# Two of 32 zero stores written in 18 pieces each, in a one-core decode kernel with gradients

## The chip, the cores and the metric

The kernel runs on one core of one Trainium2 chip. The metric is device microseconds of a whole execution; the time shown is the median of the runs. One execution was also taken by the hardware profiler, and the times of single instructions and DMAs below come from that one.

## The reference

The reference is a forward step and its gradients. A layer norm of `x` (4 batch rows of 512) feeds two branches, whose results are added to `x`: attention of one query position against a key and value cache, and a gated feed-forward layer. The program returns the sum and the gradients with respect to `x`, both caches and all five weights.

```python
def _A_ref(x, k_cache, v_cache, wq, wo):
    W = min(4096, max(256, Sk // 4))
    k = jnp.repeat(k_cache[:, :, Sk - W:, :], rep, axis=1)
    v = jnp.repeat(v_cache[:, :, Sk - W:, :], rep, axis=1)
    ...
xn = _layernorm(x, axis=-1)
return x + _A_ref(xn, A_k_cache, A_v_cache, A_wq, A_wo) + _B_ref(xn, B_w_gate, B_w_up, B_w_down)
...
_out, _vjp = jax.vjp(_f, A_x, A_k_cache, A_v_cache, A_wq, A_wo, B_w_gate, B_w_up, B_w_down)
_grads = _vjp(grad_out)
```

The caches have the shape 4 x 8 x 4096 x 128 (batch, kv-heads, positions, head size) in bfloat16. Only the last 1024 positions of each are used. The gradients of the caches have the full shape, so for the first 3072 positions they are zeros, and these zeros have to be written: 768 KB for each kv-head of each batch and cache, 64 such heads in all, of 81 MB of outputs.

## The kernel before

The kernel first does the feed-forward layer with its weight gradients, then attention batch by batch (scores against K, dP against V, the gradients of V and K, the part of the output and of dq), and last the gradients of `wo` and `wq`. Compute works on tiles in SBUF. Results are copied from PSUM into staging tiles of 1 MB (`stg`, four buffers; late in the kernel also `late` and `last`, on the place of cache tiles) and stored from there.

All large DMAs are issued by SP, in the order in which the kernel's text calls them (`manual_schedule` with `nc.sync.engine`). On that one queue stand:

- the loads of weights (lines 148 and 299 to 302), and of the caches by `load_kv` (line 259): one batch of K or V as two DMAs of 1 MB
- the result stores by `result` (line 109), of 896 KB or 1 MB
- two stores of 4 KB (line 878) for the output and the gradient of `x`
- 32 zero stores by `zeros` (line 277), of 1.5 MB each

A zero store writes the zeros of two kv-heads (`ZG = 2`) of one batch and cache. Each head is seen as 64 rows (`ZP`) of 12 KB (`ZW` = 6144 elements). The source `zsrc` is every second partition of `ztile`, a tile of zeros filled once (line 217), with a step of 0 over the heads. `ztodo` lists the stores, `zdone` those issued. `zeros(n)` issues n of them; `behind` makes each one wait for the landing of the zero store four before it.

Where zero stores stand among the others is written out by hand: `before` (line 105) gives, for each result store, how many zero stores are issued ahead of it, and lines 430, 432, 696 and 717 issue some between the loads of the caches. Numbered from 0 as in `zdone`, store 8 is issued at line 696 for batch 0, right after the two loads of V for batch 1 and ahead of the two loads of K for batch 2 (line 716). Store 29 is issued by `result` ahead of the sixth of the eight stores of weight gradients at the end. After it come that sixth store (1 MB), zero store 30, the seventh, zero store 31 and the eighth.

The framework gives SP's DMAs completion counters in turn, eight in all. An instruction that uses a counter waits until the DMA that last used it has landed, unless an earlier wait covers that.

Of the kernel before, what the change touches and what calls it, by code (L numbers as in the profile page):

```python
# [19 lines left out]
def kernel(  # L20
# [24 lines left out]
    nc = tc.nc  # L45
# [7 lines left out]
    K0 = Sk - W  # L53
# [53 lines left out]
    def result(out, in_):  # L107
        zeros(min(before.popleft(), len(ztodo)))
        return nc.sync.dma_start(out=out, in_=in_)
# [104 lines left out]
    ZP = P // 2  # L214
    ZW = K0 // ZP * Dh
# [48 lines left out]
    ZG = 2  # L264
    zsrc = bass.AP(tensor=ztile.tensor, offset=ztile.offset, ap=[[2 * ztile[:].ap[0][0], ZP], [0, ZG], [1, ZW]])
    ztodo = [(og, b, g) for b in range(B) for g in range(0, G, ZG) for og in (out_2, out_3)]
    zdone = []

    def behind(ins, other):
        tc.add_manual_dep(ins, other.name,  # L270
                          mybir.DependencyInfo(mybir.DependencyClass.Sync, mybir.DependencyReason.DATA))

    def zeros(n, after=None, deep=4):

        for _ in range(n):
            og, b, g = ztodo.pop(0)
            z = nc.sync.dma_start(out=og[b, g:g + ZG, 0:K0, :].rearrange("g (m j) d -> m g (j d)", m=ZP), in_=zsrc)
            if len(zdone) >= deep:
                behind(z.ins, zdone[-deep].ins)
            if after is not None:  # L280
                behind(z.ins, after.ins)
            zdone.append(z)
# [139 lines left out]
    with tc.tile_pool(name="mid", bufs=1, reuse_waits="tile") as mid:  # L422
# [4 lines left out]
        with (tc.tile_pool(name="kvp", bufs=1, reuse_waits="tile") as kvp,  # L427
              tc.tile_pool(name="att", bufs=1, reuse_waits="tile") as att):
            load_kv(0, 1, kvp, "va", nc.sync)
            zeros(2)  # L430
            load_kv(1, 0, kvp, "kb", nc.sync)
            zeros(3)


# [126 lines left out]
            def small(name, shape=(P, 1)):  # L561
                return att.tile(list(shape), FP32, name=name, tag=name)
# [77 lines left out]
            for b in range(B):  # L640
                S = sps[0][:]
                m = small("m")
# [122 lines left out]
            for i in range(KH):  # L765
                t, e, c = i // 8, i // 4 % 2, i % 4
# [144 lines left out]
```

## Time and profile before

| what | value |
|---|---|
| median of 3 runs | 276.65 us (276.42 to 276.9) |
| profiled execution | 276.85 us |
| its span | 275.1 us |
| busy PE, DVE, ACT, POOL | 171.7, 175.8, 122.1, 30.7 us |
| DMA | 24432 packets, 111.88 MB, mean 407 GB/s |
| HBM read, written | 30.68 MB, 81.01 MB |
| zero stores | 32 of 1.5 MB, median 18.3 us from issue to landing |
| store 8, store 29 | issued at 90.48 and 240.93 us |
| last instruction of a compute engine in the chain of waits | ends at 236.45 us |

The span is the time from the first to the last event of the profile; the execution's time has 1.75 us around it. A DMA's issue on SP is a row of its own (engine SPq); the transfer itself runs on the 16 DMA engines, and is seen in the rows of DMA share and GB/s, as packets (a row of a transfer is one packet), and in the landings. A DMA over 16 engines completes once on each of them, and has landed with the last.

### The profile page before, as it was taken

The page shows a single profiled execution, that of the slowest core. Times are in us where ns is not written, and L with a number is a line of the kernel's source. Part 1 is how long each engine was busy: PE and PEld are TensorE (multiplying, and loading weights), DVE is VectorE, ACT ScalarE, POOL GpSimd, SP SyncE. Part 2 cuts the span into 40 slices and gives each one's busy share as a digit, 9 for nine tenths or more (in the row PEclk, how much of TensorE's full clock was granted, in tenths as well). Part 3 has the DMA queues.
Part 4 walks back from the last instruction along what each step waited for, and adds up shares of the span by engine and source line. Part 5 has one row for each costly group of instructions (what it writes and reads, how often), then busy time and mean ns, then how long its engine had stood idle before and what let it go on. Part 6 is the DMA issues. An engine that isn't in the chain of part 4 may idle for free.

```text
span 275.1 us, 3144 instructions
## 1 busy us (share of the span) xinstructions
PE 171.7 (62%) x1095; PEld 57.4 (21%) x1095; DVE 175.8 (64%) x332; ACT 122.1 (44%) x246; POOL 30.7 (11%) x91
## 2 busy tenths in 40 slices
PE   1257988878247668937788778987979956200000
PEld 0121341123023212313223322341112311000000
DVE  7879669988887497515784498619996688300000
ACT  2343674940202766543675556647574455300000
POOL 8500005251152011200000000000000000000000
PEclk9985885558855955555555555555595575555555
DMA  7999989999999999999999999999999999999993
GB/s 267 435 472 401 434 338 421 429 423 403 425 403 436 407 415 415 409 412 402 406 408 433 400 417 417 429 406 431 418 420 407 417 416 429 423 424 421 421 426 152
DMA packets 24432, 111.88 MB, mean 407 GB/s; under 512 B 1361, under 2 KB 1377, under 8 KB 18785
## 3 DMA queue, kind: packets, MB, share of 16 engines
q1 hardware_dynamic: 24408, 111.69, 99.5%
q8 instruction: 8, 0.13, 0.2%
q14 instruction: 8, 0.06, 0.0%
q10 hardware_dynamic: 8, 0.00, 0.0%
HBM read 30.68 MB, written 81.01 MB: 406 GB/s over the span
## 4 chain that ended last, share of the span: by engine, by line
PE 27%; DVE 17%; ACT 7%; DMA 6%; issue 4%; DVEq 0%; ACTq 0%
DVE scr L94 8%; DMA out_dram<-stg 6%; PE kv_ps L131 5%; PE dw_ps L131 4%; PE od_ps L131 4%; PE sc_ps L131 3%; ACT stg L114 2%; PE ok_ps L131 2%; DVE dqs L728 2%; DVE stg L114 2%; ACT late L114 2%; PE dxq_ps L131 1%; DVE wq_t L94 1%; PE dn_ps L131 1%; PE ob_ps L131 1%
## 5 line engine op out<-in xcount | busy, mean ns | idle before, releaser
L114 ACT CAST stg<-kv_ps 128x512 bf16<-128x512 f32 x102 | 54.6, 601 | 41.0 <-PE kv_ps L131 34.1
L131 PE MATMUL sc_ps<-scr,bd 128*32 128x256 bf16 x256 | 19.6, 399 | 17.1 <-DVE scr L94 16.7
L131 PE MATMUL kv_ps<-qm,spr 64*128 64x512 bf16 x64 | 24.3, 582 | 2.2 <-DVE stg L114 0.8
L131 PE MATMUL kv_ps<-dyBD,spr 64*128 64x512 bf16 x64 | 20.7, 584 | 3.4 <-ACT stg L114 3.3
L94 DVE STREAM_TRANSPOSE scr<-va 128x1024 uint32<-128x1024 uint32 x16 | 19.5, 1224 | 0.0
L114 DVE CAST stg<-kv_ps 128x512 bf16<-128x512 f32 x10 | 6.6, 689 | 16.0 <-PE kv_ps L131 16.0
L131 PEld LDWEIGHTS <-spr 64*128 64x128 bf16 (+1 forms) x192 | 9.2, 106 | 29.4 <-issue 25.0
L612 DVE SCALAR_TENSOR_TENSOR odt<-od_ps,om,odt 128x128 f32<-128x128 f32 x12 | 4.2, 351 | 15.6 <-ACT odt L607 15.4
L131 PEld LDWEIGHTS <-bd 128*32 128x32 bf16 x256 | 6.3, 106 | 34.2 <-issue 33.4
L89 ACT CAST stg<-dwg_ps 128x448 bf16<-128x448 f32 x26 | 11.9, 571 | 3.0 <-DVE scr L94 1.9
L114 DVE CAST stg<-dw_ps 128x512 bf16<-128x512 f32 x16 | 10.5, 685 | 4.2 <-PE dw_ps L131 4.0
L131 PE MATMUL dw_ps<-scr,xn_b 32*128 32x512 bf16 x32 | 9.6, 546 | 5.7 <-ACT late L114 4.0
L114 ACT CAST late<-dw_ps 128x512 bf16<-128x512 f32 x16 | 9.2, 587 | 8.5 <-PE dw_ps L131 8.5
L131 PE MATMUL do_ps<-scr,dyBD 128*128 128x512 bf16 x32 | 10.6, 472 | 2.4 <-DVE scr L94 2.3
L114 DVE CAST late<-dw_ps 128x512 bf16<-128x512 f32 x16 | 10.6, 678 | 1.8 <-PE dw_ps L131 1.7
L114 ACT CAST stg<-dw_ps 128x512 bf16<-128x512 f32 x16 | 8.9, 588 | 5.9 <-PE dw_ps L131 5.3
L94 DVE STREAM_TRANSPOSE scr<-wo_sb 128x1024 uint32<-128x1024 uint32 x8 | 9.7, 1230 | 1.3 <-ACT scr L465 0.7
L94 DVE STREAM_TRANSPOSE scr<-ka 128x1024 uint32<-128x1024 uint32 x8 | 9.8, 1234 | 0.8 <-PE r_ps L131 0.7
L94 DVE STREAM_TRANSPOSE scr<-kb 128x1024 uint32<-128x1024 uint32 x8 | 9.9, 1240 | 0.1
L520 POOL COPY bd<-D3d 32x64 bf16<-32x64 bf16 x32 | 7.0, 231 | 23.7 <-DVE D3d L94 11.4
L520 POOL COPY bd<-D3q 32x64 bf16<-32x64 bf16 x32 | 7.2, 239 | 19.6 <-PE sc_ps L131 15.9
L131 PE MATMUL dw_ps<-dy_b,scr 32*128 32x512 bf16 x32 | 8.5, 528 | 1.0 <-ACT late L114 0.7
(200 smaller groups left out, 314.7 us busy)
## 6 DMA issues: line engine op xcount, KB each, us to landing
out_dram<-ztile SPq DMA_DIRECT2D x32, 1536.0 KB, 18.3
out_dram<-stg SPq DMA_DIRECT2D x18, 1024.0 KB, 16.2
va<-in_A_v_cache_dram SPq DMA_DIRECT2D x8, 1024.0 KB, 12.9
out_dram<-stg SPq DMA_DIRECT2D x6, 896.0 KB, 8.5
wq_sb<-in_A_wq_dram SPq DMA_DIRECT2D x1, 4096.0 KB
wo_sb<-in_A_wo_dram SPq DMA_DIRECT2D x1, 4096.0 KB
ka<-in_A_k_cache_dram SPq DMA_DIRECT2D x4, 1024.0 KB, 12.7
kb<-in_A_k_cache_dram SPq DMA_DIRECT2D x4, 1024.0 KB, 15.6
```

The costliest lines, as they stand in the source:

```text
L89: return nc.scalar.copy(out=out, in_=in_)
L94: nc.vector.transpose(out=out, in_=in_)
L114: return nc.scalar.copy(out=out, in_=in_) if eng == "act" else nc.vector.tensor_copy(out=out, in_=in_)
L131: nc.tensor.matmul(out, lhsT=lhsT, rhs=rhs, start=first, stop=last, **kw)
L520: nc.gpsimd.tensor_copy(out=t_[q, :, :, g2, :, o_:o_ + 4], in_=src[q, b, g2])
L612: STT(out=t_[:], in0=ps[:, g, :], scalar=(om, oms)[k][:, g:g + 1], in1=t_[:], op0=ALU.mult, op1=ALU.add)
L728: nc.vector.tensor_copy(out=dqs[q, :, :, :, a * B + b], in_=d3v[q])
```

## The change

In `zeros`, the stores that find 8 or 29 entries in `zdone` are cut. The first DMA then covers one kv-head, g, with its 64 rows of 12 KB. The other head, g + 1, is written as one contiguous stretch of 768 KB, from its start, by 17 further DMAs: 48 rows of 12 KB, 16 rows of 8.25 KB (4224 elements), and 15 DMAs of 15, 14, ... 1 rows of 512 bytes (256 elements). The bytes written are the same. The waits that `behind` adds stay on the first DMA, which is also the one noted in `zdone`. All other zero stores are as before.

```diff
             og, b, g = ztodo.pop(0)
-            z = nc.sync.dma_start(out=og[b, g:g + ZG, 0:K0, :].rearrange("g (m j) d -> m g (j d)", m=ZP), in_=zsrc)
+            cut = len(zdone) in (8, 29)
+            z = nc.sync.dma_start(out=og[b, g:g + ZG - cut, 0:K0, :].rearrange("g (m j) d -> m g (j d)", m=ZP),
+                                  in_=zsrc[:, 0:ZG - cut, :])
+            if cut:
+                head = og[b, g + 1, 0:K0, :].rearrange("k d -> (k d)")
+                at = 0
+                for n, w in [(48, ZW), (16, 4224)] + [(k, 256) for k in range(15, 0, -1)]:
+                    nc.sync.dma_start(out=head[at:at + n * w].rearrange("(m e) -> m e", m=n), in_=zsrc[0:n, 0, 0:w])
+                    at += n * w
+                assert at == ZP * ZW
             if len(zdone) >= deep:
                 behind(z.ins, zdone[-deep].ins)
```

In the built program the 17 DMAs stand on SP right behind the first one, and take the completion counters in turn like all others. The DMAs behind them move on to other counters.

## The prediction

> **What bounds the kernel now.** I read the slices of the page first, then its queues, then busy times by stretch, then SP's issues and waits.
>
> ```profile
> DMA  7999989999999999999999999999999999999993
> GB/s 267 435 472 401 434 338 421 429 423 403 425 403 436 407 415 415 409 412 402 406 408 433 400 417 417 429 406 431 418 420 407 417 416 429 423 424 421 421 426 152
> ...
> q1 hardware_dynamic: 24408, 111.69, 99.5%
> ```
>
> The 16 DMA engines are full from the second slice to the last but one, nearly all with SP's queue. No compute engine passes 64% of the span.
>
> ```profile
> core 0: us, PE busy (x) PEld busy (x) DVE busy (x) ACT busy (x) POOL busy (x), PEclk, DMA share, GB/s
> ...
> 90.00:106.00 16.00, 10.44 (x88) 3.62 (x85) 11.22 (x21) 11.15 (x24) 2.10 (x8) 0.71 1.02 410
> 106.00:122.00 16.00, 11.32 (x85) 3.98 (x84) 7.73 (x20) 7.83 (x19) 1.85 (x8) 0.50 1.04 416
> ...
> 241.00:260.00 19.00, 0.00 (x0) 0.00 (x0) 0.00 (x0) 0.00 (x0) 0.00 (x0) 0.50 1.01 424
> 260.00:268.00 8.00, 0.00 (x0) 0.00 (x0) 0.00 (x0) 0.00 (x0) 0.00 (x0) 0.50 1.00 420
> 268.00:275.00 7.00, 0.00 (x0) 0.00 (x0) 0.00 (x0) 0.00 (x0) 0.00 (x0) 0.50 0.40 167
> ```
>
> Around both changed stores the DMA share is 1.0 or above, and from 241 us on nothing but DMA runs. There is no DMA idle time in which new idle time could hide. The 0.40 of the last 7 us is the engines finishing at different times: the trace's completion records of the last store run from 269.19 to 274.26 us, 5.07 us apart. The latest engine sets the end.
>
> ```profile
> start us, us, engine line op out<-in xcount [idle before <-releaser]
> 89.14 1.29 SPq L259 DMA_DIRECT2D va<-in_A_v_cache_dram  x2
> 90.48 2.80 SPq L277 DMA_DIRECT2D out_dram<-ztile  x1
> 93.38 2.91 SPq L259 DMA_DIRECT2D ka<-in_A_k_cache_dram  x2
> 96.33 6.83 SPq L277 DMA_DIRECT2D out_dram<-ztile  x1
> ```
>
> ```profile
> 228.46 0.28 SPq L878 DMA_DIRECT2D out_dram<-scr  x1
> 231.00 0.26 SPq L878 DMA_DIRECT2D out_dram<-bd  x1
> 234.71 0.61 SPq L277 DMA_DIRECT2D out_dram<-ztile  x1
> 237.28 0.36 SPq L109 DMA_DIRECT2D out_dram<-late  x1
> 240.93 0.61 SPq L277 DMA_DIRECT2D out_dram<-ztile  x1
> 243.40 0.36 SPq L109 DMA_DIRECT2D out_dram<-late  x1
> ```
>
> ```profile
> SPq L277 <- DMA out_dram<-ztile: 14.1, 4, 4.1
> ```
>
> Counting zero stores from 0, number 8 is issued at 90.48 us and number 29 at 240.93. The last row says what SP waits for late in the kernel: landings of older zero stores. SP's DMAs use eight completion counters in turn, and in the built program each waits, before it is issued, for the landing of the DMA eight before it on the same counter. Store 29 shows it: store 26, eight DMAs earlier, landed at 240.91 us, 0.02 before the issue. So at most eight DMAs are queued. In before these are 1 MB to 1.5 MB each, some 9 MB or over 20 us of work, and the queue never runs empty.
>
> **The change, part by part.** The bytes do not change. For stores 8 and 29 each, one DMA (1.5 MB) becomes 18: 0.75 MB, 576 KB, 132 KB, and fifteen of 7.5 KB down to 0.5 KB. That is 34 more DMAs. Order and number of instructions on PE, DVE, ACT and POOL stay.
>
> *The work of the rows.* Packet records give 84 ns for a 2 KB row, 460 ns for a 12 KB row and 9 ns for a counter's increment; the line through the two rows is 9 ns + 36.7 ps per byte. I estimate from it 319 ns for 8.25 KB and 28 ns for 512 bytes. An engine's part of the old store was 8 x 460 + 9 = 3.69 us. Now its large rows cost 7 x 460 + 319 + 3 x 9 = 3.57 us, 0.12 less, and each small store that uses the engine adds 28 + 9 = 37 ns. No 512-byte row is in the trace. If it cost as much as a 2 KB row, the engine with 15 of them would have 15 x 93 = 1.40 us instead of 0.56; at no cost, 0.14. These run while the queue is otherwise empty (next part), so I count them at nothing. Without that cover the engine with all 15 is 0.56 - 0.12 = 0.44 us later per split.
>
> *The counters.* Here I expect the cost. Call the small stores by their rows, 15 to 1. Stores 15 to 10 wait for earlier large DMAs. Store 9 is on the counter of the 48-row piece and store 8 on that of the 8.25 KB piece. Both can only be issued when that piece has landed on all 16 engines. At that moment nothing large is queued: everything older has landed, and behind it stand only rows of 512 bytes. SP must still issue 8, 7, ... 1 before the next large transfer, and that one waits for store 8's landing too. The next large transfers are the ka loads for batch 2 after store 8, and the sixth weight store (`late`) after store 29.
>
> The empty time of the latest engine per split, measured against before, in which its next row follows at once: 0.12 us gained in the rows; 0.33 us from its last packet to the landing (273.93 to 274.26 at the end of the kernel); 0.02 us to wake SP; eight small issues; and the start of the next transfer. The nearest issues are the 4-row ones, 0.28 and 0.26 us at L878, with some 0.05 us between neighbours. I take 0.33 each: 8 x 0.33 = 2.6 us. The lower end is 8 x 0.31 = 2.5, the upper 8 x 0.61 = 4.9 (the 4-row load on ACT's queue took 0.56). For the start, the kernel's first load is the only one into empty engines:
>
> ```profile
> 0.80 0.39 SPq L148 DMA_DIRECT2D wg_sb<-in_B_w_gate_dram  x1
> ```
>
> ```profile
> 1.00:1.50 0.50, 0.00 (x0) 0.00 (x0) 0.00 (x0) 0.10 (x1) 0.42 (x4) 1.00 0.00 0
> ```
>
> Its first packet starts at 1.82 us: 1.0 us (0.6 after the issue ended; up to 1.4 for later engines). Sum: -0.12 + 0.33 + 0.02 + 2.6 + 1.0 = 3.85 us, from 3.3 to 6.6. A gain is excluded while the queue does run empty. The landing of store 8 can take the place of the issues: the 4-row load on ACT's queue landed 2.6 us after its issue began, just the eight issues, so it adds nothing.
>
> *The engines' lateness.* A drain lets early engines wait for the latest. At store 8's landing they are 3.50 us apart, at store 29's 5.10. After a drain all start together, and the time is the sum of the worst engine of each stretch instead of the worst sum. The latest engine gains 5.10 - 3.50 = 1.60 us between the stores; if the second latest there (2.90) is the one at 4.87 later, it gains 1.97, and the drain costs 0.37 more. I take 0.4 (0 if one engine is worst in all stretches, 1.5 if the engine at 1.76 becomes that at 4.87).
>
> *Behind the waits on SP:* ka for batch 2, then zero store 9, then the first result stores (103.27 us before), whose staging buffers ACT waits for (until 121.02 us in the chain of waits). All shift with the queue by the same 3.85 us; a second cost would need SP to run dry, and at its later issues 6 us or more of transfers are queued.
>
> *Total:* 276.85 + 2 x 3.85 + 0.4 = 284.95 us, where 276.85 us is the profiled execution (span 275.1 and 1.75 around it), 0.2 above the median of 276.65. I say 284.9.
>
> **Rivals.**
>
> *One drain is absorbed.* If the compute that runs ahead during the first drain shortens later gaps, one drain counts: 276.85 + 3.85 + 0.4 = 281.1. For it: ACT and PE run on during the first. Against: the share of 1.0 leaves no gap to shorten.
>
> *The round trips are exposed.* If a small landing into HBM takes 5 us and not 2.6 (the L878 stores took 18 and more, behind other work), the next large transfer waits 2.4 us longer per split: 284.95 + 4.8 = 289.7. Against: the engines are empty then.
>
> *Not slower: the fall evens out the engines.* If the queue stays fed, only the rows count. Were the latest engine one that gets none of the small rows, it would save 0.12 us per split: 276.85 - 0.24 = 276.6. It decides from the point where some large transfer is still queued when store 8 is issued. Were it the engine that gets all 15: 276.85 + 0.88 = 277.7. For it: the row counts 15 to 1 are a ramp over engines. Against: the order of counters; and after the store that ended at 249.47 us on its latest engine, the 4-row store of L878 ended at 249.64, so the latest engine is one of the four that it used. [...]
>
> **How the numbers follow.** Two drains 0.73 (own range 283 to 288); one absorbed 0.10; exposed round trips 0.08; queue fed, engines relieved 0.06, or loaded 0.03. The range 281 to 289.5 leaves out the two queue-fed cases and about half of the exposed one. A change under 0.2% (0.55 us) can't be told from none here. Faster 0.02 (the relief larger than worked out), same 0.05, slower 0.93.
>
> **What would show it.** In the changed profile: two dips of the DMA share, near 105 to 110 and near 263 to 267 us, each about 4 us on the latest engine; SP waiting at the small stores for landings of ztile; eight small issues in a row at about 0.33 us right ahead of ka and `late`; busy times of PE, DVE and ACT as before; completions of the last store closer together than 5.07 us. Wrong if the DMA share stays 1.0 there, if the small issues take much less than 0.3 us, or if a dip lasts past the next large issue.

## The result, and the profile after

| kernel | median | of runs | ratio to before |
|---|---|---|---|
| before | 276.53 us | 4 (276.37 to 276.90) | |
| changed | 298.60 us | 4 (298.36 to 299.13) | 1.0791 [1.0775, 1.0807] |

The change costs 22.1 us. The forecast was 284.9 us with a range of 281 to 289.5, so the sign was right and the size was short by 13.7 us. The profiled execution of the changed kernel took 298.47 us, with a span of 296.8 us, 21.7 us more than before.

The page of the changed kernel first: busy times, then the busy share of the DMA engines and GB/s in 40 equal slices (7.42 us each), then SP's queue.

```profile
PE 174.9 (59%) x1095; PEld 57.9 (19%) x1095; DVE 176.4 (59%) x332; ACT 121.9 (41%) x246; POOL 30.6 (10%) x91
...
DMA  7999999999999906999999999999999999993297
GB/s 285 431 451 425 372 407 427 430 412 398 406 436 409 360 18 204 371 421 406 404 397 432 402 418 410 427 407 438 408 425 396 427 422 423 423 411 90 99 425 327
...
q1 hardware_dynamic: 24952, 111.69, 93.4%
```

There are two holes. One begins near 104 us and one near 267 us, and between them the engines are full as before. SP's queue moves the same 111.69 MB, but its packets fill 93.4% of the span where they filled 99.5%. The compute engines do nearly the same work: DVE is busy 0.6 us longer and PE 3.2 us, of 296.8.

The same view in short stretches, with columns as in the table by stretches of the prediction (start and end, length, busy time of PE, PEld, DVE, ACT and POOL, granted clock, DMA share, GB/s):

```profile
104.00:106.00 2.00, 1.75 (x13) 0.28 (x5) 1.10 (x2) 1.30 (x3) 0.92 (x4) 0.50 0.11 37
106.00:108.00 2.00, 1.51 (x9) 0.34 (x12) 1.97 (x5) 1.07 (x3) 0.00 (x0) 0.50 0.03 8
...
110.00:112.00 2.00, 1.83 (x20) 0.74 (x12) 1.15 (x3) 2.00 (x7) 0.92 (x4) 0.50 0.01 2
112.00:114.00 2.00, 1.79 (x25) 0.53 (x17) 1.77 (x7) 2.00 (x6) 0.45 (x2) 0.50 0.09 27
114.00:118.00 4.00, 3.45 (x22) 1.39 (x23) 1.52 (x6) 0.20 (x1) 0.46 (x2) 0.50 0.95 324
118.00:122.00 4.00, 0.00 (x0) 0.00 (x0) 0.00 (x0) 0.00 (x0) 0.00 (x0) 0.93 0.99 314
266.00:270.00 4.00, 0.00 (x0) 0.00 (x0) 0.00 (x0) 0.00 (x0) 0.00 (x0) 0.50 0.83 228
270.00:274.00 4.00, 0.00 (x0) 0.00 (x0) 0.00 (x0) 0.00 (x0) 0.00 (x0) 0.50 0.09 25
274.00:278.00 4.00, 0.00 (x0) 0.00 (x0) 0.00 (x0) 0.00 (x0) 0.00 (x0) 0.50 0.02 5
278.00:282.00 4.00, 0.00 (x0) 0.00 (x0) 0.00 (x0) 0.00 (x0) 0.00 (x0) 0.50 0.48 194
```

Both holes are some 10 us wide at their base and nearly empty for over 6 us. Two further stretches matter. From 114 to 122 us the DMA engines are busy (0.95 and 0.99), yet move only 324 and 314 GB/s. From 266 to 270 us, ahead of the second hole, they move 228 GB/s at a share of 0.83. A busy share is not throughput: the 12 KB rows begun from 266 to 269 us took a mean of 758 ns, where their median before is 460, and the 2 KB rows from 118 to 122 us a mean of 120 ns, where those from 100 to 113 us before took 86.

SP's issues of the changed kernel, columns as before (start, duration with the waits in it, line, operation). L278 is the first DMA of a zero store and L284 the 17 pieces.

```profile
88.55 5.00 SPq L278 DMA_DIRECT2D out_dram<-ztile  x1
93.60 18.96 SPq L284 DMA_DIRECT2D out_dram<-ztile  x17
112.67 0.95 SPq L259 DMA_DIRECT2D ka<-in_A_k_cache_dram  x2
```

```profile
252.67 0.50 SPq L278 DMA_DIRECT2D out_dram<-ztile  x1
255.12 24.20 SPq L284 DMA_DIRECT2D out_dram<-ztile  x17
279.44 0.36 SPq L109 DMA_DIRECT2D out_dram<-late  x1
```

The pieces hold SP for 19 and 24 us, and the next large transfer is issued only behind the last of them, at 112.67 and 279.44 us. What SP waits for between 245 us and the end:

```profile
SPq L284 <- DMA out_dram<-ztile: 5.3, 3, 3.0
SPq L284 <- DMA out_dram<-stg: 3.8, 2, 1.9
```

These are landings of older DMAs, so the counters do hold back the small stores. The last wait is that of the 9-row store, for the landing of the 48-row piece: that came at 273.02 us, the issue began at 273.04. The 8.25 KB piece landed at 273.35, while this issue was still running, so the 8-row store did not have to wait for it. What comes after is not waiting but issuing. The issues of L284 from 107 to 112.5 us, with their number, shortest, median and longest duration in ns:

```profile
L284 SPq DMA_DIRECT2D out_dram<-ztile x9: 424/707/747, 106.3 to 112.1; - x9
```

A small issue takes 0.7 us. The prediction had 0.33 from one issue to the next.

From the completion records of the latest engine, the 21.7 us of the span are these. "Pieces" is the time to the landing of the 8.25 KB piece against the same bytes before; "restart" is from the issue of the next large transfer to a later landing (of zero store 9, or of the last store), against before.

| part | first cut | second cut |
|---|---|---|
| pieces | 4.58 - 3.67 = 0.91 | 6.03 - 3.70 = 2.33 |
| store of 9 rows, issued last before the eight | 0.51 | 0.48 |
| eight small issues | 112.67 - 107.07 = 5.60 | 279.44 - 273.83 = 5.61 |
| restart | 12.65 - 9.85 = 2.80 | 16.31 - 14.81 = 1.50 |
| sum | 9.82 | 9.92 |

Between the cuts another 2.20 us are lost, the start gains 0.45 and the tail loses 0.17: 9.82 + 9.92 + 2.20 - 0.45 + 0.17 = 21.7 us.

### The profile page after: what moved, and what is told of

Same layout as the page of the kernel before. It is cut to its first block, busy times and chain, and to the rows that moved or that the text cites. A ratio compares the mean times of both kernels' runs of the same rounds, so it can differ in the third digit from the quotient of the medians.

```text
span 296.8 us, 3178 instructions
## 1 busy us (share of the span) xinstructions
PE 174.9 (59%) x1095; PEld 57.9 (19%) x1095; DVE 176.4 (59%) x332; ACT 121.9 (41%) x246; POOL 30.6 (10%) x91
## 3 DMA queue, kind: packets, MB, share of 16 engines
q1 hardware_dynamic: 24952, 111.69, 93.4%
## 4 chain that ended last, share of the span: by engine, by line
PE 23%; DMA 15%; DVE 13%; ACT 6%; issue 2%; SPq 1%; ACTq 0%; DVEq 0%
DMA out_dram<-stg 15%; DVE scr L94 6%; PE dw_ps L131 5%; PE kv_ps L131 4%; PE od_ps L131 3%; PE ok_ps L131 2%; ACT stg L114 2%; DVE dqs L737 2%; DVE stg L114 2%; PE sc_ps L131 2%; ACT late L114 2%; PE dxq_ps L131 1%; PE ob_ps L131 1%; PE dn_ps L131 1%; DVE wq_t L94 1%
## 5 line engine op out<-in xcount | busy, mean ns | idle before, releaser
L131 PE MATMUL kv_ps<-dyBD,spr 64*128 64x512 bf16 x64 | 21.4, 607 | 12.1 <-ACT stg L114 12.1
L131 PE MATMUL kv_ps<-qm,spr 64*128 64x512 bf16 x64 | 25.0, 601 | 2.1 <-DVE stg L114 0.8
L89 ACT CAST stg<-dwg_ps 128x448 bf16<-128x448 f32 x26 | 11.9, 567 | 3.0 <-DVE scr L94 1.9
L114 DVE CAST late<-dw_ps 128x512 bf16<-128x512 f32 x16 | 10.8, 682 | 3.4 <-PE dw_ps L131 3.3
L131 PE MATMUL do_ps<-scr,dyBD 128*128 128x512 bf16 x32 | 10.0, 443 | 2.5 <-DVE scr L94 2.3
L131 PE MATMUL dw_ps<-dy_b,scr 32*128 32x512 bf16 x32 | 9.2, 576 | 1.0 <-ACT late L114 0.7
L529 POOL COPY bd<-D3q 32x64 bf16<-32x64 bf16 x32 | 7.2, 238 | 22.1 <-PE sc_ps L131 18.4
```

The lines of the kernel that those rows point to most:

```text
L89: return nc.scalar.copy(out=out, in_=in_)
L114: return nc.scalar.copy(out=out, in_=in_) if eng == "act" else nc.vector.tensor_copy(out=out, in_=in_)
L131: nc.tensor.matmul(out, lhsT=lhsT, rhs=rhs, start=first, stop=last, **kw)
L529: nc.gpsimd.tensor_copy(out=t_[q, :, :, g2, :, o_:o_ + 4], in_=src[q, b, g2])
```

## The experiments

In the diffs, which are shortened, `LOOP` stands for the list after `for n, w in`, and "..." for what is left out. Lines with "-" are those of the changed kernel. Ratios are to the kernel before, run on the same chip (medians 276.55 to 276.74 us).

**One cut at a time.** Are the two drains independent, or is one absorbed?

```diff
-cut = len(zdone) in (8, 29)
+cut = len(zdone) in (29,)      # only29
+cut = len(zdone) in (8,)       # only8
```

> Only store 29 is cut. Theory (each split empties the queue and then pays for itself): the second split's part of the changed kernel's trace, from the landing of the DMA before store 29 to the end, is 9.9 us longer than before, so 276.5 + 9.9 = 286.4 us. Rival (the splits are not independent: the second is dear because the first has used up lateness or buffers): clearly less than 9 or more than 11 us over before.

> Only store 8 is cut. Theory: 9.4 us up to the landing of zero store 9 and 2.2 us more by the time of store 28, because the engines are level after the drain and fall apart again: 276.5 + 11.6 = 288.1 us. Rival (the 2.2 us belong to the second split): 276.5 + 9.4 = 285.9 us.

Measured: only29 287.48 us, 1.039 [1.037, 1.0411]; only8 288.54 us, 1.0429 [1.0407, 1.045]. The costs are 10.8 and 11.9 us, and their sum of 22.7 is within 0.7 of the 22.1 of both. only29 is 1.1 us above the 286.4 expected; by the completion records of its trace 0.8 of that is its pieces, which took 3.1 us more than the same bytes before, not 2.3. Neither drain is absorbed, though PE, DVE and ACT go on working in the first.

**One DMA for all short rows.** Same rows and bytes, but 4 DMAs per cut instead of 18, so that the counters are not used up by small ones.

```diff
-LOOP = [(48, ZW), (16, 4224)] + [(k, 256) for k in range(15, 0, -1)]
+LOOP = [(48, ZW), (16, 4224), (120, 256)]     # 120 rows from ztile[0:n, 0:w]
```

> Both stores are cut, but the 120 rows of 512 bytes are one DMA, so each split has 4 DMAs and not 18. Theory (eight counters full of tiny stores empty the queue): the queue stays fed, the DMA share stays near 1, and at most the slow rows of the 48-row and 8.25 KB pieces remain (0.9 and 2.3 us): 276.5 to 279.7 us. Rival (the short rows and unequal pieces cost by themselves): 290 us or more, with the same dips.

Measured: 282.01 us, 1.0183 [1.0158, 1.0209]. The drain is gone, so the number of small DMAs makes it. But 5.3 us stay, more than the theory allowed: something in the large pieces costs time without a drain. From 254 to 258 us of the profiled execution (283.97 us, the longest of the four) the table by stretches says so (share and GB/s are the last two columns):

```profile
254.00:258.00 4.00, 0.00 (x0) 0.00 (x0) 0.00 (x0) 0.00 (x0) 0.00 (x0) 0.50 1.00 304
```

The engines are full and move 304 GB/s, where 420 is usual.

**Rows over all 16 engines.** Is a small issue slow because its rows don't divide over 16 engines? In the changed kernel's trace a store of n rows, n from 15 to 1, has n completion records; the piece of 16 rows and every larger DMA have 16.

```diff
-LOOP = ... + [(k, 256) for k in range(15, 0, -1)]
+LOOP = ... + [(16, 128)] * 15
```

> The 15 small stores of each split have 16 rows of 256 bytes each, the same bytes in all. Theory (a small store costs SP 0.7 us when it directly follows another, whatever its rows): 298.6 us within 1. Rival (the 0.7 us come from using fewer than 16 engines or a number of rows that is no power of two): the issues fall to the 0.4 us of large DMAs in a row, eight of them save 2.4 us per split, 293.8 us.

Measured: 297.52 us, 1.0753 [1.0726, 1.078]. The issues from 106 to 111.7 us:

```profile
L284 SPq DMA_DIRECT2D out_dram<-ztile x9: 508/587/1130, 105.6 to 111.1; - x9
```

Still 0.59 us each. The row count is not what makes them slow, or only 0.1 us of it.

**Small stores from neighbouring partitions.** `zsrc` steps over every second partition. Here only the small stores' source changes; number, bytes and targets stay.

```diff
-in_=zsrc[0:n, 0, 0:w]
+in_=zsrc[0:n, 0, 0:w] if n > 15 else ztile[0:n, 0:w]
```

> As the changed kernel, but the small stores read neighbouring partitions of the zero tile and not every second one. Theory (a small issue is dear because its source steps over partitions: stores from ztile issue in 0.5 to 0.6 us alone, the 120-row store with neighbouring partitions in 0.34): the issues fall from 0.70 to about 0.4 us, eight of them save 2.4 us per split, 293.8 us. Rival (back to back, the descriptor maker itself needs 0.6 to 0.7 us for each DMA): no change, 298.6 us within 0.5.

Measured: 291.65 us, 1.0538 [1.0507, 1.0568]. The issues from 106.3 to 109 us:

```profile
L285 SPq DMA_DIRECT2D out_dram<-ztile x8: 251/285/294, 106.3 to 108.6; - x8
```

An issue falls from 0.71 to 0.285 us, and eight of them take 2.64 us, just the term of the prediction. The kernel gains 7.0 us: 2 x (5.60 - 2.64) = 5.9 from the eight, the rest mostly from the ninth. The source with the step makes the slow issue; this is the largest part of what the prediction missed. The one-row store, which has no second partition to step to, still took 0.42 us against 0.25 here, so a part goes with how the source is described and not with the partitions that are read; no run separates that part. The expectation had the direction, but too small a gain.

**Half as many small stores, and the cut without a clump.** `eight15` has 8 stores of 15 rows per cut instead of 15 stores. `spread8` cuts store 8 only, and issues its small stores one at a time, each ahead of one of SP's next 15 DMAs.

```diff
-LOOP = ... + [(k, 256) for k in range(15, 0, -1)]
+LOOP = ... + [(15, 256)] * 8                  # eight15
```

```diff
+    def one_more():                           # spread8; called ahead of each later DMA on SP
+        if small_:
+            o_, i_ = small_.popleft()
+            nc.sync.dma_start(out=o_, in_=i_)
...
-                    nc.sync.dma_start(out=..., in_=zsrc[0:n, 0, 0:w])
+                    if n > 15: nc.sync.dma_start(out=one[0], in_=one[1])
+                    else: small_.append(one)
```

> The 120 rows of each split are eight stores of 15 rows and not fifteen of 15 to 1. Theory (the empty time is the issues left to SP when the last large piece lands): only the eighth small store and the next large DMA are left then, seven issues of 0.7 us less per split, 298.6 - 9.8 = 288.8 us. Rival (once the queue has run empty most of the cost is there, whatever the count): over 294 us.

> Only store 8 is cut, into the same 18 pieces, but its 15 small stores are issued one at a time ahead of SP's next 15 DMAs. Theory (small stores cost only where eight in a row fill the counters): no drain; what stays is the slow rows of the large pieces, up to half of what one_small showed, and some 0.2 us for each small store on the latest engine at the most: 277 to 281 us. Rival (each small store costs its issue and its place on a counter wherever it stands): 288 us as with the small stores in a row.

Measured: eight15 288.26 us, 1.0415 [1.0379, 1.0451]; spread8 279.4 us, 1.0091 [1.0067, 1.0115]. Both as the theory had it. SP's issues in eight15 (first row: all ten pieces) and the table by stretches of spread8:

```profile
93.92 13.33 SPq L284 DMA_DIRECT2D out_dram<-ztile  x10
107.36 1.03 SPq L259 DMA_DIRECT2D ka<-in_A_k_cache_dram  x2
```

```profile
104.00:112.00 8.00, 7.10 (x45) 2.04 (x46) 7.10 (x14) 6.54 (x15) 1.40 (x7) 0.50 1.02 404
112.00:120.00 8.00, 4.37 (x38) 1.73 (x39) 2.41 (x11) 1.38 (x5) 0.92 (x4) 0.50 1.04 414
```

With eight small stores ka goes out at 107.36 us instead of 112.67. With the same 15 small stores apart from each other the DMA share stays above 1.0 and 404 GB/s flow where the changed kernel had its hole. So the clump of small stores makes the drain, not their number, rows or slow issue. How many in a row it takes, between one and eight, was not tried.

**What is wrong with the large pieces?** Four kernels ask it. `two_heads` writes the second head as one DMA of 64 rows; `halves` cuts into two DMAs of 32 rows in both heads; `one_home` lets the 48 and the 16 rows read from 16 partitions eight apart; `shape48` writes the second head as 48 and 16 rows of 12 KB, with nothing small.

```diff
-LOOP = [(48, ZW), (16, 4224)] + [(k, 256) for k in range(15, 0, -1)]
+LOOP = [(64, ZW)]                             # two_heads
+LOOP = [(48, ZW), (16, ZW)]                   # shape48
```

```diff
+half = bass.AP(..., ap=[[4 * step, ZP // 2], [0, ZG], [1, ZW]])                # halves
+nc.sync.dma_start(out=og[b, g:g + ZG, 0:K0 // 2, :]..., in_=half)
+z = nc.sync.dma_start(out=og[b, g:g + ZG, K0 // 2:K0, :]..., in_=half)
```

```diff
+rows = bass.AP(..., ap=[[8 * step, 16], [0, 3], [1, w]])                       # one_home, 48 rows
+rows = bass.AP(..., ap=[[8 * step, 16], [1, w]])                               # one_home, 16 rows
```

> Both stores are cut into two DMAs only, one of 64 rows of 12 KB for each head; nothing small, nothing unequal. Theory (with all engines inside one head's 768 KB, the writes get in each other's way): rows of 500 to 1500 ns around both stores and 2 to 5 us over before, 279 to 282 us. Rival (the 48-row and 8.25 KB shapes are at fault, or the small rows): 276.7 us within 0.4.

> Both stores are cut into two DMAs, each with 32 rows of 12 KB in both heads, so that every DMA spans two heads as in before. Theory (one head at a time is what slows the rows): 276.7 us within 0.4. Rival (any cut of a store, or a source with other partitions, does it): as two_heads.

> [...] Theory (the 48- and 16-row pieces are slow because several engines read the same few partitions): the slow rows go, 276.7 to 277.5 us. Rival (they are slow by where they write or by unequal pieces): 282 us as before.

> Both stores are cut into 64 rows of 12 KB for one head, and 48 and 16 rows of 12 KB for the other; no row is short. Theory (16 engines read 48 or 16 rows out of fewer partitions than in the 64-row stores, and so get in each other's way): rows of 600 to 1500 ns around both stores, 279 to 282 us. Rival (the rows of 512 bytes are what slows the others): 276.9 us within 0.5, as two_heads.

Measured: two_heads 277.08 us, 1.002 [1.001, 1.0029]; halves 276.73 us, 1.0008 [0.9998, 1.0017]; one_home 282.19 us, 1.02 [1.0158, 1.0243]; shape48 282.19 us, 1.0207 [1.0181, 1.0233]. A second large DMA costs next to nothing, so the theory for two_heads fell. The same 64 rows as 48 + 16 cost 5.6 us with no small store in the kernel. The tables by stretches of shape48, then of two_heads:

```profile
248.00:252.00 4.00, 0.00 (x0) 0.00 (x0) 0.00 (x0) 0.00 (x0) 0.00 (x0) 0.50 1.01 424
252.00:256.00 4.00, 0.00 (x0) 0.00 (x0) 0.00 (x0) 0.00 (x0) 0.00 (x0) 0.50 1.04 355
256.00:260.00 4.00, 0.00 (x0) 0.00 (x0) 0.00 (x0) 0.00 (x0) 0.00 (x0) 0.50 0.99 341
```

```profile
252.00:256.00 4.00, 0.00 (x0) 0.00 (x0) 0.00 (x0) 0.00 (x0) 0.00 (x0) 0.50 1.00 418
256.00:260.00 4.00, 0.00 (x0) 0.00 (x0) 0.00 (x0) 0.00 (x0) 0.00 (x0) 0.50 1.00 421
```

Both are full, at 341 and at 421 GB/s: the rows of shape48 themselves are slower. one_home was meant to mend this and failed: that the slow rows would go was worked out from the author's assumption of which engine reads which partitions, and no trace here shows that. Its packets tell more: 29 of the 202 rows of 12 KB from 251 to 263 us took 905 to 971 ns, twice the usual 460, and from 255 to 259 us it moved 288 GB/s at a share of 0.97. one_small writes the same rows to the same places from other partitions, and there 9 of 196 rows took 900 to 1000 ns and 16 longer, up to 2281. So the times of the rows changed with the partitions that they are read from. In halves, whose 32 partitions lie four apart over all 128, no 12 KB row from 248 to 262 us took over 500 ns. Why 48 and 16 rows from every second partition are slow (341 GB/s in shape48) and so are the rows from 16 partitions eight apart (288 GB/s in one_home), while 64 from every second (421 GB/s in two_heads) and 32 from every fourth are not, is not shown. Nor does any run keep the number of rows and change their partitions to reach the usual rate, so a part that the number of rows in a DMA has by itself is not ruled out.

**The large pieces from 64 partitions.** `rows64one` is one_small with the large pieces as 64 rows of 9 KB and 64 rows of 2.1 KB; `unit64` is unit with the same pieces.

```diff
-LOOP = [(48, ZW), (16, 4224)] + ...
+LOOP = [(64, 4608), (64, 1056), (120, 256)]                                   # rows64one
+LOOP = [(64, 4608), (64, 1056)] + [(k, 256) for k in range(15, 0, -1)]        # unit64
```

> As one_small, with the 48 rows of 12 KB as 64 of 9 KB and the 16 of 8.25 KB as 64 of 2.1 KB, so that all large rows come from the partitions of an uncut store; the 120 rows of 512 bytes stay one DMA. Theory (few source partitions): 276.9 us within 0.6. Rival (the 512-byte rows): 281 to 282.5 us as one_small.

> As with neighbouring partitions for the small stores, and the large pieces as 64 rows each. Theory (the pieces' slow rows cost 1.5 to 2.4 us of the 15 that are left): 289.7 us, 0.8 either way. Rival (the slow rows come with the small ones): 291.6 us within 0.5.

Measured: rows64one 277.38 us, 1.0033 [1.002, 1.0046]; unit64 288.59 us, 1.0435 [1.0414, 1.0455]. In place of the 304 GB/s of one_small, rows64one shows

```profile
254.00:258.00 4.00, 0.00 (x0) 0.00 (x0) 0.00 (x0) 0.00 (x0) 0.00 (x0) 0.50 1.01 403
```

and loses 0.8 us instead of 5.3. Within the drained kernel the shape is worth 291.65 - 288.59 = 3.1 us, more than expected by 1.1. In unit64's own completion records the pieces take 3.64 and 3.66 us, where the same bytes took 3.67 and 3.70 before, and the eight issues 2.67 and 2.64. What unit64 still loses, 12.0 us, is the drain at the issue price of the prediction.

**The large pieces over both heads.** `clean` wrote the large pieces over both heads at once (64 and 96 rows), 16 rows beside them, and the small stores from neighbouring partitions.

```diff
+z = both_heads(0, K0 // 2, 32)
+both_heads(K0 // 2, K0 - 240, 48)
+nc.sync.dma_start(out=og[b, g, K0 - 240:K0, :]..., in_=zsrc[0:16, 0, 0:1920])
...
+for n in range(15, 0, -1):
+    nc.sync.dma_start(out=..., in_=ztile[0:n, 0:256])
```

> Both stores are cut into 18 pieces, but the large pieces span both heads and the 15 small stores read neighbouring partitions. Theory (what is left is the drain as the prediction worked it out, 2.6 + 1.3 us per split, with the slow loads of 1.5 and the engines falling apart again for 2.2 us): 276.7 + 7.8 + 3.7 = 288.2 us, 1 either way. Rival (the pieces' shapes never mattered): 291.7 us as with neighbouring partitions alone.

Measured: 291.3 us, 1.0532 [1.0511, 1.0553], the rival's number. It still reads 48 and 16 partitions, and so doesn't separate the shape from the rest; unit64 was made for that.

**The slow loads after the first drain.** In the changed kernel the two ka loads, 2 MB, took 7.9 us from first packet to landing, where 5.3 is usual on most engines (6.2 on the latest engine for the same two loads before). `swap8` cuts store 8 only and issues zero store 9 ahead of ka.

```diff
-    load_kv(b + 2, 0, ...)
     zeros(1 - b)
+    load_kv(b + 2, 0, ...)
```

> Only store 8 is cut, as in only8, and zero store 9 stands ahead of the two ka loads behind the split. Theory (loads of 2 KB rows are slow while all engines run level after the drain: 8 us for 2 MB instead of 5.3): the loads stay slow behind a zero store, 288.5 us within 0.7. Rival (only the first transfer into the empty engines is slow): the loads take 5.3 us, some 1.5 to 2.5 us less in all, 286 to 287 us.

Measured: 289.05 us, 1.0451 [1.043, 1.0471]. The total is the one expected, but not for the reason given: the ka loads ran at 2.74 and 2.73 us per MB, nearly as usual, and now zero store 9 took 5.6 us from first packet to landing instead of 3.7 (these times from the first packet hold some 0.3 us from the last packet to the landing, which the usual ones, from landing to landing, do not). So it is not the loads: the first 1.5 to 2 MB after the first drain are slow, whatever they are. After the second drain the rows of the 1 MB store of `late` took their usual 0.31 us. Compute goes on during the first drain and not during the second, but it does not explain this: from 118 to 122 us of the changed kernel no compute engine is busy, and the rate is still 314 GB/s. The cause stays open.

## Why the prediction was right in kind and wrong in size

- **The counters.** Right. The small stores wait for landings, nothing large stands behind them, the DMA engines run empty twice, and SP then issues eight small stores before the next large transfer. spread8 and one_small take the clump away and with it the drain.
- **The step that failed: "I take 0.33 each: 8 x 0.33 = 2.6".** A small issue took 0.70 us and the eight 5.60, beyond even the upper end of 4.9 given for them. The row it was taken from, a 4-row store from neighbouring partitions, was the wrong neighbour: in unit, with such sources, the eight took 2.64 us as predicted, against 5.60 from every second partition. The signs were in the same timeline: zero stores, which read the same `zsrc`, were issued in 0.61 us, and the 1 MB stores of `late` in 0.36. That row was quoted and used only as a bound. Worth 3.0 us per cut, and 0.5 more for the ninth store, which SP issues when the large pieces are nearly or wholly done. The unit run puts both at 7.0 us. With these 7.0 the sum would have been 292 us, still 6.6 short: three smaller parts, below, were short or missing.
- **The rows of the large pieces: "0.12 less" per cut.** Also failed, and wrong in sign. The 319 ns from the line through 2 KB and 12 KB rows is the median of the 8.25 KB rows (mean 371, up to 1187), but the 12 KB rows from 266 to 269 us, the 48-row piece and what ran beside it, took a mean of 758 ns and not 460. shape48 shows 5.6 us for the shape alone; in the drained kernel it is 3.1 us (unit to unit64). That the empty time hides the difference is the author's reading of these two numbers; no run shows it by itself.
- **The 512-byte rows.** Right: a median of 31 ns (27 to 100, 240 rows) against 28. A small store costs the latest engine some 0.18 us with its completion, not 0.037, but hidden in the drain, as was said: at the second cut the last completions of the 8.25 KB piece and of the stores of 15 to 10 rows stand at 273.35, 273.54, 273.72, 273.90, 274.09, 274.28 and 274.46 us.
- **The restart, 1.0 us.** Right: ka's first packet starts at 113.73 us, 1.07 after its issue began. The second cut's restart of 1.50 us is the 1.35 of the prediction (1.0 + 0.33 + 0.02). The first cut's 2.80 has 1.5 us more, the slow first transfers, which the prediction didn't have.
- **The lateness, 0.4 us.** Right in kind, too small, and beyond its upper end of 1.5: the engines leave the first drain level (0.48 us apart at the landing of zero store 9), fall apart again to 2.79 at store 28, and 2.20 us are lost on the way. The mean of the 16 engines took only 0.34 us longer over this stretch than before, so it is the latest engine that loses.
- **The claim that the latest engine is one of the four of a 4-row store** fits before, where it was read (four completion records, the last at 249.64 us), and does not hold in the changed kernel: there the last completion of these stores is at 259.11 us, that of the large DMA ahead of them only at 261.20. That one engine gets a row of all 15 small stores (the 0.56 and 0.44 us, and the 277.7) was the author's assumption; the trace has no engine numbers, only the number of completion records.
- **A small slip in the sum.** The terms of the 3.85 as printed add up to 3.83. It changes the forecast by less than 0.1 us.

The prediction's two drains were to cost 8.1 us. The runs add 7.0 for the source step and 3.1 for the shape; with 12.0 left in unit64 that is 22.1, as it must be, since these are differences of the same medians. Of the 3.9 us by which 12.0 exceeds 8.1, the traces put some 1.5 on the slow first transfers and about 2 on lateness; no run separates these two.

The rivals: one drain absorbed (281.1) fell with only8. The exposed round trips (289.7) fell too: the time is in issues, not in waits for small landings (the 8-row store issued at 107.07 us had landed at 108.80, after 1.73 us; no run shows the 5 us of that rival). The queue that stays fed (276.6 or 277.7) is what rows64one shows, at 277.38 us, but for one small DMA and not for fifteen. What was to show the steps did, but for the issues at 0.33 us and the length of the dips: there are the two dips, busy compute nearly as before, and the last store's completions 0.18 us apart instead of 5.07.

No version beats the kernel before; halves is equal to it.

## What to carry to other kernels

When a queue's DMAs share a few completion counters, count a run of tiny DMAs against the number of counters. Here fifteen in a row emptied the queue (a DMA share of 0.11 and less from 104 to 112 us), and the cost was the time to issue the last ones plus a restart (5.60 and 2.80 us at the first cut). Eight in a row, as many as there are counters, still cost 11.5 us for two cuts (eight15), and fifteen set apart among large ones 2.7 us for one (spread8), both with the slow rows of the large pieces in the cost. Price an issue from a row with the same source pattern, not with the same size (0.285 us from neighbouring partitions in unit, 0.71 from every second one in the changed kernel). When a store's rows are regrouped, ask from which partitions they are read at one time: a full busy share at a lower GB/s (0.99 at 341 in shape48) was the sign of it here.

## What the hardware showed that was not expected

- SP's issue of a store went with the source's pattern far more than with its bytes: 0.25 to 0.30 us for one to eight 512-byte rows from neighbouring partitions (unit), 0.60 to 0.74 for two to eight from every second one (0.42 for a single row; the changed kernel), 0.59 for 16 rows of 256 bytes from every second one (sixteen), 0.61 for a zero store of 1.5 MB and 0.36 for a store of 1 MB of `late` (before).
- 12 KB rows took a median of 460 ns from 64 partitions spread over all 128 (before), a mean of 758 from 266 to 269 us in the changed kernel (the 48-row piece and what ran beside it), and 905 to 971 in many rows of one_home (16 partitions eight apart).
- After the first drain the first 1.5 to 2 MB took some 40% longer, a load or a store alike (7.9 us instead of 5.3, 5.6 instead of 3.7, each with 0.3 us to the landing in the longer time). After the second they did not. The cause is open.
